# Attention in fixed program order, three units in flight, and weight requests next to the sums that free their buffers

## Chip, cores, metric

One core of one Trainium2 chip. The metric is the time of one execution on the device, in microseconds (us), as the median of several runs. Kernels of one call run on the same chip and share the runs of the kernel before.

## The reference

```python
def phi(x):                                   # 64 -> 256 features
    proj = einsum('bhsd,df->bhsf', x, w_phi)
    proj = proj - max(abs(proj), axis=-1)
    return concatenate([exp(proj), exp(-proj)], axis=-1)
q_p, k_p = phi(q), phi(k)                     # 8 batches, 8 heads, 576 rows, 64 columns
kv  = einsum('bhsf,bhsd->bhfd', k_p, v);  z = sum(k_p, axis=2)
x   = (q_p @ kv) / (q_p @ z + 1e-6)           # -> (8, 576, 512)
X   = rfft(x, axis=1)[:, :64]                 # 64 modes
Y   = X * (w_r + i w_i)                       # one 512x512 complex matrix for each mode
u   = x + irfft(Y, n=576)
out = u + relu(u @ w_ch)
```

The weights `w_r` and `w_i` are 134 MB of fp32 in HBM. They are cast to bf16 on the way in, so 67 MB land.

## The kernel before

Attention runs in 16 units: 4 groups `g` of two heads, times 4 pairs `bp` of batches. When a group's four units are done, its 128 channels are in frequency form, and 16 "sums" (calls of `mix`) of four modes each can run. There are 64 sums, and each consumes one weight tile of 2 x 512 KB. So the first sum can run only after unit 3.

```python
pw_cm  = tc.tile_pool(name="pw", bufs=7)      # weight tiles, 1 MB each
pin_cm = tc.tile_pool(name="pin", bufs=2)     # q, k, v of a unit
pm_cm  = tc.tile_pool(name="pm", bufs=2)

def load(g, bp):                              # 12 DMA requests
    ...
    for t, src, eng in ((kb, k, nc.gpsimd), (vn, v, nc.sync), (qb, q, nc.gpsimd)):
        for i in range(2):
            hs = src[2 * bp + i, 2 * g:2 * g + 2]
            eng.dma_start(t[:, 8*i:8*i+8, :]..., hs[:, 0:512, :].rearrange("h (p c) d -> p h (c d)", c=4))
            eng.dma_start(t[64*i:64*i+64, 16:18, :], hs[:, 512:576, :].rearrange("h p d -> p h d"))

def keys(st):       # transpose k, project, abs-max (DVE), two exponentials (ACT), weigh v (DVE), key sums (PE)
    ...
def queries(st, XT): # the same for q, then numerator and denominator, then the forward transform into XT
    ...
def wload(g, mg):
    wt = pw.tile([128, 2, MG, DMODEL], BF16, name="wt", tag="wt")
    for i, w in ((0, moe_w_r), (1, moe_w_i)):
        nc.gpsimd.dma_start(wt[:, i], w[mg*MG:(mg+1)*MG, g*128:(g+1)*128, :].rearrange("m p e -> p m e"))
    return wt

for n, u in enumerate(units):
    g, bp = u
    if n + 2 < len(units):
        st[units[n + 2]] = load(*units[n + 2])
    next_w(2 if g == 0 else 3)                # ask for two or three weight tiles
    if n + 1 < len(units):
        keys(st[units[n + 1]])
    ...
    queries(st.pop(u), XTb[g % 2])
    for _ in range(3):                        # three sums a unit, once there are any
        if mixq:
            mix(*key, wts.pop(key), ...)
    ...
# after attention: one sum, one weight request and two "channel" chunks (x @ w_ch) a turn;
# then the output stage
```

The scheduler decides the order of each engine's instructions. It need not be the program's.

Of the kernel before, what the change touches and what calls it, by code (L numbers as in the profile page):

```python
# [20 lines left out]
NG = 4  # L21
# [5 lines left out]

@with_exitstack
def kernel(
# [13 lines left out]
    nc = tc.nc  # L43

# [20 lines left out]
    pw_cm = tc.tile_pool(name="pw", bufs=7)  # L65
# [7 lines left out]
    def load(g, bp):  # L73
        kb = pin.tile([128, 18, D_], BF16, name="kb")
        qb = pin.tile([128, 18, D_], BF16, name="qb")
        vn = pin.tile([128, 18, D_], F32, name="vn")
        for t, src, eng in ((kb, k, nc.gpsimd), (vn, v, nc.sync), (qb, q, nc.gpsimd)):
            for i in range(2):
                b = 2 * bp + i
                hs = src[b, 2 * g:2 * g + 2]  # L80
                eng.dma_start(  # L81
                    t[:, 8 * i:8 * i + 8, :].rearrange("p (h c) d -> p h (c d)", h=2),
                    hs[:, 0:512, :].rearrange("h (p c) d -> p h (c d)", c=4),
                )
                eng.dma_start(
                    t[64 * i:64 * i + 64, 16:18, :],
                    hs[:, 512:576, :].rearrange("h p d -> p h d"),
                )
        return dict(g=g, bp=bp, qb=qb, kb=kb, vn=vn)


    wpf = const.tile([128, 128], F32, name="wpf")
    nc.sync.dma_start(wpf[0:64, :], w_phi)
    nc.sync.dma_start(wpf[64:128, :], w_phi)
    si = const.tile([128, 5], I32, name="si")
    nc.gpsimd.iota(si[:, 0:4], [[1, 4]], base=0, channel_multiplier=4)
    nc.gpsimd.iota(si[0:64, 4:5], [[1, 1]], base=512, channel_multiplier=1)
    nc.gpsimd.iota(si[64:128, 4:5], [[1, 1]], base=512, channel_multiplier=1)
    mi = const.tile([128, 64], I32, name="mi")
    nc.gpsimd.iota(mi, [[4, 2], [8, NO], [1, 4]], base=0, channel_multiplier=0)  # L100

    st = {(0, 0): load(0, 0)}
# [4 lines left out]
    nc.vector.tensor_copy(ident_b, ident_f)  # L107
    w2blk = const.tile([128, 256], BF16, name="w2blk")
    nc.vector.memset(w2blk, 0.0)
    nc.vector.tensor_copy(w2blk[0:64, 0:128], wpf[0:64, :])  # L110
    nc.vector.tensor_copy(w2blk[64:128, 128:256], wpf[64:128, :])

    CF = const.tile([128, 6, 4, 64], BF16, name="CF")
# [3 lines left out]
    nc.vector.tensor_copy(sf, si)  # L117
    mf = const.tile([128, 64], F32, name="mf")
    nc.vector.tensor_copy(mf, mi)

    def sc(i):
        return yacc[:, 2 * i:2 * i + 2, :].rearrange("p a e -> p (a e)")[:, 0:640].rearrange(
            "p (c r m) -> p c r m", c=5, r=2)

    ang, rnd, csf = sc(0), sc(1), sc(2)
    nc.vector.tensor_tensor(
# [5 lines left out]
    nc.vector.tensor_scalar_add(out=ang[:, :, 0, :], in0=ang[:, :, 1, :], scalar1=S_ / 4.0)  # L132
    MAGIC = 8388608.0
    nc.vector.tensor_scalar(
        out=rnd, in0=ang, scalar1=1.0 / S_, scalar2=MAGIC, op0=ALU.mult, op1=ALU.add)
    nc.vector.tensor_scalar(
        out=rnd, in0=rnd, scalar1=-MAGIC, scalar2=-float(S_), op0=ALU.add, op1=ALU.mult)
    nc.vector.tensor_tensor(out=ang, in0=ang, in1=rnd, op=ALU.add)
    nc.scalar.activation(csf, ang, ACT.Sin, scale=2.0 * math.pi / S_)

    def tables():

        nc.vector.memset(CF[:, 4:6], 0.0)
        for p0, p1, d, n in ((0, 128, 0, 4), (0, 64, 4, 1), (64, 128, 5, 1)):
            src = csf[p0:p1, min(d, 4):min(d, 4) + n]
            dst = CF[p0:p1, d:d + n]
            nc.vector.tensor_copy(dst[:, :, 0, :], src[:, :, 0, :])
            nc.vector.tensor_scalar_mul(out=dst[:, :, 1, :], in0=src[:, :, 1, :], scalar1=-1.0)
            nc.vector.tensor_copy(dst[:, :, 2, :], src[:, :, 1, :])
            nc.vector.tensor_copy(dst[:, :, 3, :], src[:, :, 0, :])  # L150

        cio = yacc[:, 6:8, :].rearrange("p a e -> p (a e)")[:, 0:640].rearrange(
            "p (c m t r) -> p c m t r", c=5, t=2, r=2)
        for r in range(2):
            for t in range(2):
                nc.vector.tensor_scalar_mul(
                    out=cio[:, :, :, t, r], in0=csf[:, :, r, 32 * t:32 * t + 32],
                    scalar1=(2.0 - 4.0 * r) / S_)
        for c in range(5):
            nc.vector.tensor_scalar_mul(  # L160
                out=cio[:, c, 0, 0, :], in0=cio[:, c, 0, 0, :], scalar1=0.5)
            pct = one([128, 128])
            nc.tensor.transpose(pct, cio[:, c].rearrange("p m t r -> p (m t r)"), ident_f)
            nc.vector.tensor_copy(CI[:, c, :], pct)

    def transposed(src, name):

        dst = pm.tile([128, 9, 128], BF16, name=name, tag="xT")
        flat = src.rearrange("p n d -> p (n d)")
        ptr = two([128, 9, 128], BF16)  # L170
        for j in range(9):
            nc.tensor.transpose(ptr[:, j, :], flat[:, j * 128:(j + 1) * 128], ident_b)  # L172
        nc.scalar.copy(dst, ptr)  # L173
        return dst

    def absmax(tT, m, by_head):

        for i in range(2):
            ps = two([128, 8, 128])
            for j in range(4):  # L180
                if by_head:
                    o = ps[:, 2 * j:2 * j + 2, :]
                else:
                    h, cc = j // 2, j % 2
                    o = ps.rearrange("p (c h) f -> p c h f", h=2)[:, 2 * cc:2 * cc + 2, h, :]
                nc.tensor.matmul(o, lhsT=tT[:, 4 * i + j, :],  # L186
                                 rhs=w2blk.rearrange("p (c f) -> p c f", c=2),
                                 start=True, stop=True)
            nc.vector.tensor_reduce(  # L189
                out=m[:, 8 * i:8 * i + 8], in_=ps, axis=AX.X, op=ALU.max,  # L190
                apply_absolute_value=True,
            )
            yield i, ps
        ps = one([128, 2, 128])
        nc.tensor.matmul(
            ps.rearrange("p h f -> p (h f)"), lhsT=tT[:, 8, :], rhs=w2blk,
            start=True, stop=True,
        )
        nc.vector.tensor_reduce(
            out=m[:, 16:18], in_=ps, axis=AX.X, op=ALU.max, apply_absolute_value=True,  # L200
        )
        yield 2, ps

    def keys(st):
        kT = transposed(st["kb"], "kT")
        mk = pm.tile([128, 2, 18], F32, name="mk")
        ABs = [pm.tile([128, 2, 8, 128], BF16, name="AB", tag="AB", bufs=3) for _ in range(2)]
        ABr = pm.tile([128, 2, 2, 128], BF16, name="ABr")
        for i, ps in absmax(kT, mk[:, 1], True):
            dst = ABs[i] if i < 2 else ABr  # L210
            nc.scalar.activation(dst[:, 0], ps, ACT.Exp, scale=1.0)  # L211
            nc.scalar.activation(dst[:, 1], ps, ACT.Exp, scale=-1.0)  # L212
        nc.vector.tensor_scalar_mul(out=mk[:, 0], in0=mk[:, 1], scalar1=-1.0)
        ee = pm.tile([128, 2, 18], F32, name="ee")
        nc.scalar.activation(ee, mk, ACT.Exp)
        va = pm.tile([128, 2, 18, 65], BF16, name="va")
        nc.vector.tensor_copy(va[:, :, :, 64], ee)
        for ab in range(2):
            nc.vector.tensor_tensor(  # L219
                out=va[:, ab, :, 0:64], in0=st["vn"],  # L220
                in1=ee[:, ab, :].unsqueeze(2).to_broadcast([128, 18, 64]), op=ALU.mult,
            )
        kvz = pm.tile([128, 2, 4, 65], BF16, name="kvz")
        for i in range(2):
            pk = one([128, 4, 65])
            for h in range(2):
                for ab in range(2):
                    o = pk[:, 2 * h + ab, :]
                    for c in range(4):
                        nc.tensor.matmul(  # L230
                            o, lhsT=ABs[i][:, ab, 4 * h + c, :],
                            rhs=va[:, ab, 8 * i + 4 * h + c, :],
                            start=(c == 0), stop=False,
                        )
                    r = slice(64 * i, 64 * i + 64)
                    nc.tensor.matmul(  # L236
                        o, lhsT=ABr[r, ab, h, :], rhs=va[r, ab, 16 + h, :],
                        start=False, stop=True,
                    )
            nc.scalar.copy(kvz[:, i], pk)  # L240
        st["kvz"] = kvz

    def queries(st, XT):
        g, bp, kvz = st["g"], st["bp"], st["kvz"]
        qT = transposed(st["qb"], "qT")
        mq = pm.tile([128, 18], F32, name="mq")
        for _ in absmax(qT, mq, False):
            pass
# [166 lines left out]
    for n, u in enumerate(units):  # L415
# [6 lines left out]
        if n == 0:  # L422
            tables()
# [93 lines left out]
```

## Time and profile before

| stage (us) | what runs | DMA landed |
|---|---|---|
| 30 to 76 | attention, first weights | 213 GB/s |
| 76 to 138 | attention alone, all seven weight buffers full | 61 GB/s |
| 138 to 364 | attention with three sums a unit | 188 GB/s |
| 364 to 503 | the other 28 sums, waiting for weights | 207 GB/s |
| 503 to 550 | output | 206 GB/s |

The median is 545.87 us (544.34 to 549.05, 3 runs).

From the page of the kernel before: the busy share of each of 40 equal slices in tenths (DMA), what the DMA engines moved, and the two DMA queues that matter. POOL issues q0 (q, k and the weights) and SP issues q1 (v and the output). The last column is the time that the packets took, as a share of 16 engines' span.

```profile
span 550.3 us, 8008 instructions
DMA  9699993343999999999999999799999999995466
GB/s 166 87 225 204 215 140 60 64 49 65 206 189 210 135 218 178 160 213 180 214 218 215 181 181 184 117 204 206 206 206 206 212 216 213 215 213 99 163 267 267
q0 software_dynamic: 94736, 77.09, 90.0%
q1 hardware_dynamic: 17568, 21.04, 12.6%
```

The hole in slices 5 to 9 is the stretch from 76 to 138 us. The next view is the busy time of each engine in given stretches of the kernel before. It ends with the granted share of the TensorE clock, the DMA share and the GB/s. A DMA share above 1 means that packets overlap on an engine: in full stretches it is 1.22 to 1.27.

```profile
core 0: us, PE busy (x) PEld busy (x) DVE busy (x) ACT busy (x) POOL busy (x), PEclk, DMA share, GB/s
30.00:76.00 46.00, 32.77 (x279) 23.31 (x279) 27.38 (x49) 26.61 (x42) 20.65 (x30) 0.81 1.27 213
76.00:138.00 62.00, 44.25 (x412) 30.25 (x413) 37.61 (x63) 34.53 (x56) 18.26 (x28) 0.67 0.41 61
138.00:364.00 226.00, 164.80 (x1631) 108.14 (x1643) 143.37 (x243) 132.45 (x205) 90.26 (x129) 0.76 1.16 188
364.00:503.00 139.00, 86.28 (x562) 37.49 (x566) 25.39 (x51) 29.55 (x51) 34.08 (x46) 0.82 1.22 207
503.00:550.30 47.30, 38.38 (x160) 15.42 (x160) 25.01 (x37) 22.29 (x38) 0.00 (x0) 0.86 0.54 206
```

Between 76 and 138 us no engine is full: PE is busy 44 of 62 us, DVE 38, ACT 35. The units wait on the chain through the engines. The chain of work that ended last, in order of time (start, duration, what), shows it there for the kernel before:

```profile
113.25 1.11 DVE mk L189
114.39 1.02 ACT AB L211
115.41 0.66 ACT AB L212
...
119.31 1.02 ACT qT L173
120.38 1.03 PE two L186 x4
```

After attention the same chain is weight DMA alone:

```profile
364.12 0.73 POOL wt L327
364.85 19.23 DMA wt<-in_moe_w_i_dram
384.37 20.05 DMA wt<-in_moe_w_i_dram
404.70 20.05 DMA wt<-in_moe_w_i_dram
```

### The profile page before, as it was taken

The page shows a single profiled execution, that of the slowest core. Times are in us where ns is not written, and L with a number is a line of the kernel's source. Part 1 is how long each engine was busy: PE and PEld are TensorE (multiplying, and loading weights), DVE is VectorE, ACT ScalarE, POOL GpSimd, SP SyncE. Part 2 cuts the span into 40 slices and gives each one's busy share as a digit, 9 for nine tenths or more (in the row PEclk, how much of TensorE's full clock was granted, in tenths as well). Part 3 has the DMA queues.
Part 4 walks back from the last instruction along what each step waited for, and adds up shares of the span by engine and source line. Part 5 has one row for each costly group of instructions (what it writes and reads, how often), then busy time and mean ns, then how long its engine had stood idle before and what let it go on. Part 6 is the DMA issues. An engine that isn't in the chain of part 4 may idle for free.

```text
span 550.3 us, 8008 instructions
## 1 busy us (share of the span) xinstructions
PE 376.5 (68%) x3103; PEld 221.7 (40%) x3133; DVE 279.7 (51%) x486; ACT 256.5 (47%) x403; POOL 186.8 (34%) x273
## 2 busy tenths in 40 slices
PE   2377767658667666778768677787766774345995
PEld 1255545445445444455445354343333331111342
DVE  7647485584555764566965665662222220000574
ACT  3346555655565566567665565312221331011463
POOL 8853331133432715626242533143223222200000
PEclk9999575775675897678975777799989996565899
DMA  9699993343999999999999999799999999995466
GB/s 166 87 225 204 215 140 60 64 49 65 206 189 210 135 218 178 160 213 180 214 218 215 181 181 184 117 204 206 206 206 206 212 216 213 215 213 99 163 267 267
DMA packets 112341, 98.63 MB, mean 179 GB/s; under 512 B 17968, under 2 KB 110768, under 8 KB 111280
## 3 DMA queue, kind: packets, MB, share of 16 engines
q0 software_dynamic: 94736, 77.09, 90.0%
q1 hardware_dynamic: 17568, 21.04, 12.6%
q8 instruction: 24, 0.39, 0.3%
q14 instruction: 13, 0.11, 0.1%
HBM read 163.64 MB, written 9.44 MB: 314 GB/s over the span
## 4 chain that ended last, share of the span: by engine, by line
PE 41%; DMA 23%; ACT 18%; DVE 12%; issue 4%; POOL 2%; DVEq 0%; POOLq 0%; ACTq 0%
DMA wt<-in_moe_w_i_dram 15%; DMA wt<-in_moe_w_r_dram 8%; PE two L186 7%; PE one L230 6%; ACT AQ L263 5%; PE one L236 5%; PE one L344 5%; ACT AB L211 4%; PE pt L466 3%; ACT AB L212 3%; PE one L283 3%; DVE mk L189 3%; PE one L312 3%; PE pt L468 3%; ACT qT L173 2%
## 5 line engine op out<-in xcount | busy, mean ns | idle before, releaser
L327 POOL DMA_DIRECT2D wt<-in_moe_w_r_dram x64 | 48.9, 764 | 93.3 <-PE one L344 37.4
L263 ACT ACTIVATE AQ<-two 128x1024 bf16<-128x1024 f32 x64 | 61.6, 1027 | 14.8 <-PE two L186 6.1
L327 POOL DMA_DIRECT2D wt<-in_moe_w_i_dram x64 | 49.0, 765 | 48.7 <-DMA wt<-in_moe_w_i_dram 44.7
L81 POOL DMA_DIRECT2D kb<-in_k_dram x32 | 23.6, 736 | 78.4 <-PE one L283 32.7
L394 ACT CAST xw<-one 128x512 bf16<-128x512 f32 x36 | 21.1, 585 | 62.0 <-PE one L392 54.9
L230 PE MATMUL one<-va,AB 128*128 128x65 bf16 x512 | 48.2, 231 | 2.6 <-DVE va L219 2.6
L392 PE MATMUL one<-wchb,xT 128*128 128x512 bf16 x137 | 39.7, 408 | 13.9 <-DVE xT L389 13.5
L186 PE MATMUL two<-w2blk,qT 128*128 128x256 bf16 x128 | 30.2, 386 | 26.4 <-ACT qT L173 26.3
L211 ACT ACTIVATE AB<-two 128x1024 bf16<-128x1024 f32 x32 | 32.9, 1028 | 31.4 <-DVE mk L189 24.6
L283 PE MATMUL one<-kvz,AQ 128*128 128x65 bf16 x512 | 35.2, 226 | 15.5 <-ACT AQ L263 13.8
L344 PE MATMUL one<-wt,XT_70 128*32 128x512 bf16 x256 | 28.7, 524 | 24.1 <-DMA wt<-in_moe_w_i_dram 14.4
L189 DVE TENSOR_REDUCE mk<-two 128x8 f32<-128x1024 f32 x32 | 42.1, 1493 | 4.7 <-PE two L186 4.7
L389 DVE COPY xT<-one 128x512 bf16<-128x512 bf16 x36 | 15.3, 424 | 56.4 <-PE one L387 56.3
L219 DVE TENSOR_TENSOR va<-vn,ee 128x1152 bf16<-128x1152 f32 x32 | 42.0, 1356 | 0.0
L189 DVE TENSOR_REDUCE mq<-two 128x8 f32<-128x1024 f32 x32 | 38.9, 1218 | 4.2 <-PE two L186 4.0
L283 PEld LDWEIGHTS <-AQ 128*128 128x128 bf16 x512 | 28.8, 120 | 28.4 <-ACT AQ L263 22.9
L312 PE MATMUL one<-CF,xs 128*128 128x256 bf16 x160 | 30.0, 309 | 13.1 <-DVE xs L303 12.1
L81 POOL DMA_DIRECT2D qb<-in_q_dram x32 | 23.4, 731 | 43.5 <-PE two L172 24.3
L230 PEld LDWEIGHTS <-AB 128*128 128x128 bf16 x512 | 32.4, 119 | 10.5 <-issue 3.2
L212 ACT ACTIVATE AB<-two 128x1024 bf16<-128x1024 f32 x32 | 33.0, 1032 | 0.0
L344 PE MATMUL one<-wt,XT_69 128*32 128x512 bf16 x256 | 26.5, 465 | 7.0 <-DMA wt<-in_moe_w_i_dram 5.8
L172 PE MATMUL two<-ident_b,kb 128*128 128x128 bf16 x144 | 18.1, 280 | 19.0 <-DVE ident_b L107 8.4
(136 smaller groups left out, 716.5 us busy)
## 6 DMA issues: line engine op xcount, KB each, us to landing
wt<-in_moe_w_r_dram POOLq DMA_DIRECT2D x64, 512.0 KB, 14.5
wt<-in_moe_w_i_dram POOLq DMA_DIRECT2D x64, 512.0 KB, 16.2
vn<-in_v_dram SPq DMA_DIRECT2D x32, 256.0 KB, 6.7
out_dram<-of SPq DMA_DIRECT2D x8, 1024.0 KB, 3.9
kb<-in_k_dram POOLq DMA_DIRECT2D x32, 128.0 KB, 5.5
qb<-in_q_dram POOLq DMA_DIRECT2D x32, 128.0 KB, 5.8
vn<-in_v_dram SPq DMA_DIRECT2D x32, 32.0 KB, 7.3
XT_69<-yst SPq DMA_DIRECT2D x8, 128.0 KB, 6.1
```

The source lines that it names most:

```text
L81: eng.dma_start(t[:, 8 * i:8 * i + 8, :].rearrange("p (h c) d -> p h (c d)", h=2), hs[:, 0:512, :].rearrange("h (p c) d -> p h (c d)", c=4),)
L186: nc.tensor.matmul(o, lhsT=tT[:, 4 * i + j, :], rhs=w2blk.rearrange("p (c f) -> p c f", c=2), start=True, stop=True)
L189: nc.vector.tensor_reduce(out=m[:, 8 * i:8 * i + 8], in_=ps, axis=AX.X, op=ALU.max, apply_absolute_value=True,)
L211: nc.scalar.activation(dst[:, 0], ps, ACT.Exp, scale=1.0)
L212: nc.scalar.activation(dst[:, 1], ps, ACT.Exp, scale=-1.0)
L219: nc.vector.tensor_tensor(out=va[:, ab, :, 0:64], in0=st["vn"], in1=ee[:, ab, :].unsqueeze(2).to_broadcast([128, 18, 64]), op=ALU.mult,)
L230: nc.tensor.matmul(o, lhsT=ABs[i][:, ab, 4 * h + c, :], rhs=va[:, ab, 8 * i + 4 * h + c, :], start=(c == 0), stop=False,)
L263: nc.scalar.activation(AQ[:, ab], ps, ACT.Exp, scale=1.0 - 2.0 * ab)
L283: nc.tensor.matmul(pn[ab][:, n - n0, :], lhsT=AQs[i][:, ab, c % 2, 2 * h + c // 2, :], rhs=kvz[:, i, 2 * h + ab, :], start=True, stop=True,)
L312: nc.tensor.matmul(px[:, :, i, :], lhsT=xs[:, g, bp, n:n + 2, :].rearrange("p h d -> p (h d)"), rhs=CF[:, c if c < 4 else 4 + i], start=(c ...
L327: nc.gpsimd.dma_start(wt[:, i], w[mg * MG:(mg + 1) * MG, g * 128:(g + 1) * 128, :].rearrange("m p e -> p m e"),)
L344: nc.tensor.matmul(py[32 * j:32 * j + 32, :], lhsT=XT[:, s0:s0 + 4, :, 32 * t + 4 * o + j].rearrange("p r b -> p (r b)"), rhs=wt[:, i, j, ...
```

## The change

The intent is threefold. Attention is cut into small steps and written in a fixed order on every engine. In step `n` the queries of unit n, the keys of unit n+1 and the transposes of unit n+2 are interleaved, so that a producer and its consumer have other work between them. Weight tiles are asked for right behind the sum that frees their buffer. The stock of weights before the first sum also grows from 7 to 13: an eighth pool buffer, and five tiles in memory that is not in use yet. The code calls those five `held`; I call them borrowed homes below.

```diff
+class InOrder:                                  # each call is kept in program order
+    def __getattr__(self, name):
+        ...
+            return self.tc.keep_in_program_order(ins) if self.on else ins
+pe, dve, act = (InOrder(tc, e) for e in (nc.tensor, nc.vector, nc.scalar))
+pool, sp = InOrder(tc, nc.gpsimd), InOrder(tc, nc.sync)
-    pw_cm = tc.tile_pool(name="pw", bufs=7)
+    pw_cm = tc.tile_pool(name="pw", bufs=8)
 ...
+    def home(g, mg):                             # the five borrowed homes
+        if g == 0 and mg < 2:            t = yacc...            # accumulator of the sums
+        elif g == 0 and mg == 2:         t = XTb[1]...
+        elif g == 0 and mg in (10, 11):  t = xs[:, mg - 8]...   # attention output of groups 2, 3
+        else:
+            return pw.tile([128, 2, MG, DMODEL], BF16, name="wt", tag="wt")
 ...
+    def some(n):
+        for _ in range(n):
+            if mixq:
+                key = mixq.pop(0)
+                mix(*key, wts.pop(key), XTb[key[0] % 2])
+                ...
+                if key not in held:
+                    next_w(1)                    # the request behind its sum
+    for n in range(-1, len(units) + 1):
+        P, Q, K, R = (unit(n + i) for i in (-1, 0, 1, 2))
+        X = 0 if n < 4 else 6 if n == 4 else 4 if n % 2 else 2    # sums in this step: 42 in all
+        Q.cols_q(0); Q.exp_q(0); K.rows_k(0); K.exp_k(0)          # (tests for None cut)
+        Q.kv(0); Q.kv(1); Q.cols_q(1); Q.exp_q(1); P.freq(); Q.num(0)
+        K.turn_q(); unit(n + 3).load_q(); K.rows_k(1); K.exp_k(1)
+        next_w(2) if n < 3 ...; some(min(X, 2)); Q.num(6); Q.cols_q(2); Q.exp_q(2); some(min(X - 2, 2))
+        K.rows_k(2); K.exp_k(2); K.weigh_v(); K.rows_q(0); K.rows_q(1); K.rows_q(2)
+        R.turn_k(); unit(n + 4).load_k(); K.weigh_v2(); unit(n + 3).load_v(); Q.num(12); K.exp_mq()
+        if n == -1: forward_table()
+        if n == 0:  inverse_table()
+        ...; some(X - 4)
-            rl = pb.tile([128, DMODEL], F32, name="rl", bufs=3)
+            rl = pb.tile([128, DMODEL], F32, name="rl")
```

Cut: the methods of a unit, which hold the same operations as `keys` and `queries` before. Only the copy out of a transpose is new: it is split in two. Some buffer counts and memories differ as well (three buffers instead of two for a transposed q or k, the transposes in smaller PSUM tiles, one buffer for `va`), and the first loads are issued in another order.

## The prediction

> **What bounds the kernel now.** The 16 DMA engines are the resource to fill. The page gives 98.63 MB moved at a mean of 179 GB/s; the busy-time table by stretch gives 205 to 215 GB/s wherever the DMA share saturates (425 to 478 us: 213). Weights are read as fp32 and land as bf16, so 213 GB/s landed is about 426 GB/s read. The Trainium skill, page "DMA: Bandwidth & Descriptors", section "Specifications", gives a fabric ceiling of 435 GB/s; the trace agrees, so I take 213 as the limit.
>
> Stages (chain of waits in order of time, and the table by stretch):
> - 0 to 364 us: attention with 36 of 64 weight sums. From 76 to 138 us DMA moves only 61 GB/s: all seven weight buffers are full and no sum can run before unit 4. Attention takes 20.7 us a unit there, although DVE is busy 12 to 13, ACT 12 and PE 15 us of it. From 138 us on, about 21.5 us a unit at 188 GB/s.
> - 364 to 503 us: the other 28 sums, 5.0 us each, waiting for DMA (207 GB/s).
> - 503 to 550 us: output, PE busy 38 of 47 us. The diff only shrinks one pool there.
>
> **What the change does.** Arithmetic and bytes stay. Every engine follows program order; step n works on the queries of unit n, the keys of n+1 and the transposes of n+2, with independent work between producer and consumer, so the unit should fall toward its busiest engine, 16.5 to 18.5 us. Stock before the first sum rises from 7 MB to 13 MB (8 pool buffers, 5 borrowed homes). A weight request stands right behind the sum that frees its buffer; sums within attention rise from 36 to 42, requests from at most 43 to 50. Added: each transpose's eviction is split in two (two 1.15 us evictions a unit become four, estimated +0.4 us ACT a unit), off the critical path if DMA bounds.
>
> **Critical path, as an estimate.** The stock moves 6 MB into the idle stretch, 6/0.213 = 28 us of DMA time. Units 4 to 15 need 3 weights plus 1.18 MB of q, k, v each: 4.2 MB/0.213 = 19.7 us against 21.5, some 20 us more. Floor: about 87.5 MB before the output at 213 GB/s is 411 us, plus 3 us start, 5 us last sum, 47 us output: 466 us. In-order PE stalls, POOL blocked on one buffer, and 206 instead of 213 GB/s in the channel stage will cost about 15 us: attention ends near 342 to 350 us, the last weight lands near 428, end near 481.
>
> **Predicted: 481 us**, range 463 to 504. Faster by over 2%: 0.96; within 2%: 0.03; slower: 0.01.
>
> **Signs.** Right: the 61 GB/s hole is gone, at least 190 GB/s in nearly every slice from 30 us to the output; first sums near 95 to 105 us; unit period 17 to 18 us early, about 20 later; the wait stretch after attention 75 to 90 us instead of 139; output still 46 to 48 us. The granted clock may rise above 0.6 in early units, since the skill's page "TensorE: Matmul & The Clock Gate", Part 1, says activity releases the throttle. Wrong: units over 20 us early, or DMA holes inside attention.
>
> **What would make it wrong.** The fixed order may stall PE behind a late exponential or a weight, holding units at 21 us: then about 500. POOL's single order may hold q and k behind a weight request. Or the output stage slows with two buffers instead of three.

## The result, and the profile after

The changed kernel takes 488.78 us (487.16 to 492.07, 4 runs) against 547.46 us for the kernel before in the same runs. The ratio is 0.893, with a 95% interval of 0.884 to 0.902. A ratio here is the mean time of one kernel's fast runs over that of the other's of the same rounds, so it is not quite the ratio of the medians.

The same lines of the page, of the changed kernel:

```profile
span 488.5 us, 8037 instructions
DMA  9999999999999999999999999999999999992576
GB/s 170 193 216 216 203 214 206 200 203 155 218 218 213 143 205 213 183 204 207 210 190 176 218 165 205 206 207 206 207 206 214 213 213 217 213 214 45 226 296 252
q0 software_dynamic: 94736, 77.09, 100.5%
q1 hardware_dynamic: 17568, 21.04, 14.5%
```

The hole is gone but for a dip from 108 to 120 us. DMA is at 90% or more from the second slice until the output stage, and the mean rises from 179 to 202 GB/s. The start is better too: the second slice moves 193 GB/s instead of 87. The stretches of the changed kernel:

```profile
30.00:76.00 46.00, 29.95 (x293) 21.17 (x294) 32.82 (x64) 27.05 (x46) 20.25 (x29) 0.78 1.27 210
76.00:138.00 62.00, 48.69 (x540) 34.21 (x544) 51.05 (x85) 45.07 (x80) 33.07 (x49) 0.88 1.23 196
138.00:325.00 187.00, 139.06 (x1474) 96.19 (x1483) 132.49 (x219) 115.84 (x197) 78.48 (x112) 0.79 1.21 197
325.00:442.00 117.00, 76.70 (x528) 34.98 (x539) 24.33 (x51) 29.31 (x51) 26.72 (x36) 0.92 1.22 209
442.00:488.50 46.50, 37.57 (x161) 15.22 (x163) 25.22 (x37) 22.56 (x38) 0.00 (x0) 0.87 0.55 209
```

In the same 62 us, 76 to 138, DVE does 51 us of work instead of 38, and DMA moves 196 GB/s instead of 61. The last unit's frequency form is written at 327.5 us (before: 366.1 us).

The lines of the chain that ended last in the changed kernel show two things. Early, it goes through the compute engines, one unit after the other. From about 217 us on it is DMA, inside attention too: even a k load stands in the queue behind weights for 12.7 us.

```profile
37.51 2.62 DVE va L38 x3
...
62.91 2.63 DVE va L38 x3
...
80.44 2.62 DVE va L38 x3
...
97.40 2.63 DVE va L38 x3
...
222.23 21.39 DMA wt<-in_moe_w_i_dram
...
248.54 12.67 DMA kb<-in_k_dram
...
266.89 21.75 DMA wt<-in_moe_w_i_dram
```

(`va` is v weighed by the keys, once a unit. L38 is the line of the in-order helper, so all attention has that line.) Of the first nine distances from one `va` to the next, eight are 16.8 to 18.8 us; one is 25.4 us, between the first two lines of this fence. The last six are 18.2 to 20.4 us and, where PE waits for k, 26.8 us.

**What the packets cost.** The bytes are the same in both kernels, yet the rate inside attention, 197 GB/s, is below that of pure weights, 206, at the same DMA share. Counting the trace's packets of the changed kernel by size explains it:

```
landed size, what          packets   mean ns   sum over 16 engines, us
 128 B  q, k tails (cast)     8192     31.8      16.3
 512 B  q, k (cast)          16384     60.7      62.2
1024 B  weights, w_ch (cast) 66048     98.8     407.9
 256 B  v tails               4096     29.0       7.4
1024 B  v, and y and z       10240     58.0      37.1
2048 B and 8192 B  output     1536      -        24.2
```

A cast packet reads twice what lands. By bytes read, the packets of 256 B, 1 KB and 2 KB take about 30, 60 and 99 ns. So a packet costs some 20 ns plus 37 to 40 ns a KB (the output's 8 KB packets, 321 ns, fit too; its 2 KB packets, 114 ns, lie above), and q and k are dear for their bytes. Without the output the sum is 538 us of 16 engines, with some 6 us of 4-byte packets (18 ns each) that the table leaves out. (The two lines of the page say the same: 115.0% of 488.5 us, less 24 us.) At the overlap of 1.24 that DMA reaches when it is full (the median of 2 us pieces before the last weight lands) that is 433 us. With 3 us of start and 46 us from the last weight to the end, this is an estimated floor of 482 us, and the changed kernel is 6 us above it. The estimate leans on the overlap: with 1.22, the mean from 30 to 442 us, it would be 490 us, so the 6 us are no firm number. The same sum from the trace of the kernel before (540 us of 16 engines, 47 us of output) gives 486 us, and that kernel is some 60 us above.

### The profile page after: what moved, and what is told of

It is laid out like the page before. It is cut to its first block, busy times and chain, and to the rows that moved or that the text cites. A ratio compares the mean times of both kernels' runs of the same rounds, so it can differ in the third digit from the quotient of the medians.

```text
span 488.5 us, 8037 instructions
## 1 busy us (share of the span) xinstructions
PE 347.6 (71%) x3104; PEld 212.3 (43%) x3133; DVE 284.4 (58%) x492; ACT 256.8 (53%) x435; POOL 181.7 (37%) x267
## 4 chain that ended last, share of the span: by engine, by line
DMA 40%; DVE 23%; PE 22%; ACT 5%; issue 4%; POOL 3%; another core or an unknown queue 0%; DVEq 0%; SPq 0%; ACTq 0%; POOLq 0%
DMA wt<-in_moe_w_i_dram 28%; PE one L38 12%; DMA wt<-in_moe_w_r_dram 9%; DVE va L38 6%; DVE mq L38 4%; PE pt L596 4%; DVE nd L38 4%; DVE mk L38 4%; DMA kb<-in_k_dram 3%; DVE xs L38 3%; PE two L38 3%; POOL wt L38 3%; PE pt L598 3%; ACT AB L38 2%; DVE rd L38 1%
## 5 line engine op out<-in xcount | busy, mean ns | idle before, releaser
L38 ACT ACTIVATE AB<-two 128x1024 bf16<-128x1024 f32 x64 | 62.1, 1022 | 50.7 <-DVE mk L38 50.3
L38 ACT ACTIVATE AQ<-two 128x1024 bf16<-128x1024 f32 x64 | 62.5, 1038 | 18.0 <-PE two L38 12.3
L38 POOL DMA_DIRECT2D wt<-in_moe_w_r_dram x59 | 44.7, 758 | 66.8 <-DMA wt<-in_moe_w_r_dram 29.1
L38 POOL DMA_DIRECT2D qb<-in_q_dram x64 | 42.2, 666 | 73.4 <-DMA wt<-in_moe_w_i_dram 31.1
L38 POOL DMA_DIRECT2D wt<-in_moe_w_i_dram x59 | 44.5, 754 | 53.9 <-DMA wt<-in_moe_w_i_dram 48.8
L38 PE MATMUL one<-va,AB 128*128 128x65 bf16 x512 | 45.8, 223 | 17.5 <-DVE va L38 17.3
L38 POOL DMA_DIRECT2D kb<-in_k_dram x64 | 42.3, 672 | 38.3 <-DMA wt<-in_moe_w_i_dram 17.9
L38 DVE TENSOR_REDUCE mk<-two 128x8 f32<-128x1024 f32 x32 | 39.0, 1219 | 5.8 <-PE two L38 5.8
L38 DVE TENSOR_TENSOR va<-vn,ee 128x1152 bf16<-128x1152 f32 x32 | 42.0, 1355 | 0.0
L38 PEld LDWEIGHTS <-AB 128*128 128x128 bf16 x512 | 29.1, 112 | 27.3 <-DVE va L38 11.9
L38 DVE TENSOR_REDUCE mq<-two 128x8 f32<-128x1024 f32 x32 | 37.7, 1217 | 1.4 <-PE two L38 1.4
L38 PE MATMUL one<-kvz,AQ 128*128 128x65 bf16 x512 | 29.6, 205 | 6.9 <-ACT kvz L38 2.7
L38 PE MATMUL one<-ident_b,kb 128*128 128x128 bf16 x144 | 14.4, 244 | 25.3 <-DMA kb<-in_k_dram 24.4
L38 PEld LDWEIGHTS <-AQ 128*128 128x128 bf16 x512 | 25.7, 105 | 15.1 <-issue 12.1
L38 PE MATMUL one<-CF,xs 128*128 128x256 bf16 x160 | 30.9, 364 | 1.7 <-DVE xs L38 1.7
L38 PE MATMUL one<-wt,XT_70 128*32 128x512 bf16 x256 | 22.5, 427 | 13.0 <-DMA wt<-in_moe_w_i_dram 8.9
L38 DVE TENSOR_TENSOR nd<-one,nd 128x390 f32<-128x390 f32 x48 | 27.1, 565 | 5.4 <-PE one L38 0.5
L609 DVE TENSOR_TENSOR of<-pt,rl 128x512 f32<-128x512 f32 x32 | 21.8, 690 | 13.8 <-ACT rl L607 13.4
L38 PE MATMUL two<-w2blk,qT 128*128 128x256 bf16 x128 | 19.8, 289 | 13.0 <-ACT AB L38 10.6
```

The source lines that it names most:

```text
L38: ins = f(*args, **kwargs)
L609: nc.vector.tensor_tensor(out=o, in0=ps[0], in1=rl, op=ALU.add)
```

## The experiments

Theory A: the DMA engines are the limit, so the time is the packets' time plus the output stage, plus whatever time they stand idle before the last weight. Theory B: the pace of the compute engines sets the time, and DMA follows. Beside these two there are the parts of the change: fixed order, step structure, stock, and place of the request.

| run | median us | ratio to before, 95% interval |
|---|---|---|
| after_again (control) | 489.21 | 0.892 (0.886 to 0.899) |
| stock8 | 509.87 | 0.929 (0.921 to 0.937) |
| late_request | 490.68 | 0.894 (0.889 to 0.899) |
| no_tails | 476.61 | 0.869 (0.864 to 0.874) |
| free_order | 492.09 | 0.895 (0.889 to 0.900) |
| before_fixed | 820.18 | 1.490 (1.479 to 1.501) |
| before_stock12 | 548.48 | 0.992 (0.982 to 1.002) |
| before_sums4 | 529.41 | 0.967 (0.961 to 0.973) |
| before_half | 502.86 | 0.914 (0.906 to 0.921) |
| after_half | 456.41 | 0.834 (0.830 to 0.839) |
| big_kv | 478.75 | 0.874 (0.868 to 0.880) |
| big_kv_tables | 471.32 | 0.862 (0.859 to 0.864) |

### after_again: the control

> Control: the changed kernel once more, on the chip of the other runs of this call. All theories: 488 us, ratio to before 0.885 to 0.90. Theory A (the DMA engines are full, so the time is the DMA packets' time plus the output stage) and theory B (the pace of the compute engines sets the time, and DMA follows) differ only in the other runs.

As expected: 489.21 us.

### stock8: without the borrowed homes

```diff
-        if g == 0 and mg < 2:          # and likewise for mg == 2 and mg in (10, 11)
+        if g < 0 and mg < 2:
-    held = [(0, mg) for mg in (0, 1, 2, 10, 11)]
+    held = []
-            next_w((2, 2, 2, 2)[n + 1]) ... next_w((1, 2, 0)[n + 1])
+            next_w((2, 2, 1, 0)[n + 1]) ... next_w((1, 0, 0)[n + 1])
```

> The changed kernel without the five borrowed homes: 8 weights in stock before the first sum, not 13; nothing else moved. Theory A: the DMA work asked for before the first sum (8 weights at 5.1 us, q, k and v of some 7.5 units at 5.8 us) is 84 us, the first sums come near 105 us, so DMA stands idle for 15 to 20 us that nothing gives back: 503 to 508 us, with a hole near 90 to 105 us in the profile. Theory B: no sum waits for a weight, 488 us, unchanged.

Measured: 509.87 us, 21 us over the control. The stretches of this run show the hole where theory A put it:

```profile
30.00:76.00 46.00, 31.34 (x277) 21.55 (x276) 30.50 (x60) 26.03 (x44) 18.71 (x28) 0.70 1.22 196
76.00:112.00 36.00, 27.96 (x282) 19.16 (x280) 28.55 (x47) 25.52 (x44) 12.24 (x19) 0.76 0.43 67
112.00:341.00 229.00, 164.20 (x1764) 113.45 (x1760) 156.47 (x260) 137.63 (x236) 98.79 (x141) 0.78 1.24 204
```

At a share of 0.43 instead of 1.24, 36 us lose 24 us of DMA time, and 21 of them show in the time. Theory B, which foresaw no change, fails here.

### late_request: requests at the end of the step

```diff
                 if key not in held:
-                    next_w(1)
+                    owed.append(key)
 ...
         some(X - 4)
+        next_w(len(owed)); owed.clear()
```

> The changed kernel with all weight requests of a step gathered at the step's end instead of each behind its sum; order, stock and sums unchanged. If asking next to the sum matters, requests come on average half a step (8 us) later and in bursts, and DMA runs dry between bursts: 495 to 505 us. If the up to 4 MB already in the queue cover it: within 1% of 488 us. Theory B: 488 us.

Measured: 490.68 us, no difference to the control that these runs resolve. But the queue does not cover the delay everywhere. From 108 to 120 us, around the first sums, DMA's share falls to 0.52 (first line), where the control only dips to 0.96 (second line):

```profile
108.00:120.00 12.00, 9.89 (x129) 7.55 (x131) 9.16 (x17) 10.06 (x19) 5.12 (x9) 0.93 0.52 61
108.00:120.00 12.00, 9.94 (x113) 6.50 (x112) 11.45 (x20) 8.81 (x18) 8.00 (x12) 0.88 0.96 136
```

That is 4 us of DMA time by these shares, of which 1.5 us shows in the medians. So the place of the request is worth little time here, although DMA does feel it.

### no_tails: the smallest packets taken away (wrong result)

```diff
-            eng.dma_start(t[64*i:64*i+64, 16:18, :], hs[:, 512:576, :]...)     # for q and k
+        dve.memset(t[:, 16:18, :], 0.0)
```

> The changed kernel without the 64-row tails of q and k (1.05 MB landed, 8192 packets of 128 bytes; zeroes in their place, so a wrong result on purpose). In the trace these packets take 16.3 us of 16 engines, at the 1.24-fold overlap of the saturated stretches 13 us. Theory A with the cost per packet: 475 us. Theory A with the cost per byte (213 GB/s): 483 us. Theory B: 487 to 488 us.

Measured: 476.61 us, 12.6 us under the control (relative error 0.024, as meant). The cost per packet said 13 us, the cost per byte 5. One per cent of the bytes took 2.6% of the time. That it is so close to 13 is partly luck: all packets together fell by 21 us of 16 engines, or 17 us of DMA time, and a hole took some of it back:

```profile
104.00:116.00 12.00, 10.93 (x123) 7.63 (x123) 8.28 (x17) 9.12 (x15) 2.61 (x4) 0.80 0.36 75
```

The run also takes away 64 small requests and the time that POOL needs to issue them, which it does not separate from the packets. The Trainium skill, page "DMA: Bandwidth & Descriptors", section "Issuing engines are not separate DMA queues", says that DMAs of all issuing engines run on the same 16 engines and interleave; that is why v's packets, which SP issues, stand in the same sum. No run here tests it across issuers: q, k and the weights all come from POOL.

### free_order: the new program, order left to the scheduler

```diff
-        self.tc, self.engine, self.on = tc, engine, True
+        self.tc, self.engine, self.on = tc, engine, False
```

> The changed program without the fixed order: the scheduler places the instructions of each engine as it did in the kernel before; steps, stock and request points as in the program. If the step structure and the stock are what count: within 2% of 488 us. If the fixed order is what holds the units at 17.5 us: the scheduler pulls producers and consumers together again, units near 20 us and DMA holes, 500 to 515 us.

Measured: 492.09 us, ratio 0.895 against the control's 0.892, with intervals that overlap almost wholly. The two kernels' instructions do differ in order on PE, DVE, ACT and POOL. The units take as long (19.3 us on average in both, from the first `va` to the last), and DMA stays full from 76 to 138 us:

```profile
76.00:138.00 62.00, 50.88 (x573) 35.95 (x574) 45.39 (x80) 46.70 (x79) 32.15 (x47) 0.83 1.23 198
```

So the fixed order is not what brings the gain; any effect is below what these runs resolve.

### before_fixed: the old program, order fixed

```diff
+    fixed.tensor, fixed.vector, fixed.scalar, fixed.gpsimd, fixed.sync = (
+        InOrder(tc, e) for e in (real.tensor, real.vector, real.scalar, real.gpsimd, real.sync))
```

> The kernel before with its attention in fixed program order on every engine, and nothing else of the change. Its program puts each consumer right behind its producer, so PE should stand waiting for ACT and DVE: units of 28 us or more, 600 us or more. If fixed order alone brought the gain: under 520 us.

Measured: 820.18 us. The longest waits of this run (engine, what it was about to do, what it waited for: us in total, times, longest):

```profile
POOL wt L38 <- PE one L38: 372.6, 18, 43.4
...
DVE mk L38 <- PE two L38: 162.9, 16, 15.9
PE one L38 <- DVE va L38: 112.3, 32, 6.3
...
PE two L38 <- DMA kb<-in_k_dram: 77.5, 20, 10.2
```

The program of before puts each consumer right behind its producer. Only a scheduler that reorders it makes it usable. A second cause is POOL, whose order is fixed too: it stands before weight requests that wait for sums, and PE waits 77.5 us in all for k. The run does not separate the two. Fixed order is bearable once the program is written in interleaved steps; by itself it costs half as much again.

### before_stock12: the old attention with the larger stock

```diff
+    def home(g, mg): ...                   # the borrowed homes of the changed kernel
-        next_w(2 if g == 0 else 3)
+        next_w(0 if n == 4 else 3)         # 12 weights in the first four units
```

> The kernel before with five borrowed homes as well as its seven buffers: 12 weights asked for in the first four units instead of 8; attention and its scheduling as before. Theory A: the idle DMA stretch of 76 to 138 us is filled with about 5 MB, 5 times 5.1 us: 516 to 525 us. Theory B: 546 us, since the units keep their 20.7 us and no sum comes earlier.

Measured: 548.48 us, no gain that these runs resolve. Theory A as I had put it fails here: it promised 516 to 525 us. The stretches of this run:

```profile
76.00:108.00 32.00, 23.92 (x231) 16.63 (x231) 19.30 (x35) 18.64 (x29) 14.26 (x22) 0.69 1.24 203
108.00:160.00 52.00, 35.48 (x327) 24.07 (x328) 31.25 (x53) 30.50 (x46) 15.67 (x23) 0.67 0.53 83
160.00:200.00 40.00, 30.23 (x301) 20.35 (x304) 25.11 (x42) 22.18 (x37) 15.60 (x24) 0.74 1.08 178
200.00:230.00 30.00, 19.15 (x174) 12.58 (x173) 15.49 (x26) 18.86 (x28) 10.80 (x17) 0.72 0.59 83
230.00:364.00 134.00, 100.18 (x1010) 64.18 (x1017) 89.75 (x155) 74.04 (x115) 50.05 (x71) 0.80 1.15 188
364.00:503.00 139.00, 84.92 (x544) 36.74 (x553) 24.52 (x49) 30.06 (x52) 32.66 (x44) 0.81 1.20 204
```

The old hole is filled until 108 us, and then it opens again at 108 to 160 and at 200 to 230 us. A sum whose weight lies in a borrowed home frees no pool buffer. After the homes are used up, requests can be ahead of the sums only by the seven buffers, and the sums keep the pace of the old attention. The requests bear it out. In the kernel before, 84 of the 128 half tiles had been asked for when attention ended at 366 us; in this run too, 84 (74 in the pool and 10 in the homes) by 364 us. From the last frequency form to the last sum it takes 136 us in both (366.1 to 502.4, 364.0 to 500.4). So the stock was given back before attention ended.

This edit has a mistake. Unit 4 writes its frequency form into `XTb[1]` before the sum that reads the weight tile (0, 2) from there: in the trace the write is at 132.2 us, and six of that sum's eight matmuls come after it, at 132.9 us and later. So one of the 64 sums is wrong. It stays within the tolerance, as the whole of before_half does with half of its weights wrong. It costs that sum a wait of 2.6 us and changes no request. before_sums4 has the same mistake; the changed kernel, where that sum runs at 110.1 us and unit 4 writes at 126.1 us, does not.

### before_sums4: larger stock and four sums a unit, old attention

```diff
-        next_w(0 if n == 4 else 3)
+        next_w(3 if n < 4 else 1 if n == 4 else 4)
-        for _ in range(3):                 # sums a unit
+        for _ in range(4):
-        for _ in range(2):                 # channel chunks a sum, after attention
+        for _ in range(3):
```

> The kernel before with the 12-weight stock and four sums a unit instead of three from unit 4 on (48 within attention instead of 36), requests to match, three channel chunks a sum in the stage after; attention and scheduler as before. The stock alone gave nothing, and I think because requests during attention cannot outrun sums, and sums keep the old pace. If that is so, more sums must let the DMA run full through attention (attention end near 375 us, 16 sums left): 490 to 510 us, without any fixed order or new step structure. If the old attention's pace itself is what costs, the added PE work only slows it: 540 us or more.

Measured: 529.41 us, 17 to 18 us below the kernel before, between the two expectations. From 156 to 384 us DMA moves 198 GB/s at a share of 1.21, so more sums do let it run nearly full. But the hole at 108 to 156 us (88 GB/s) stays, since the first sum (126.5 us) still comes only when the fourth old unit is done, and the first sums use borrowed homes. This fits both parts of the reading: requests must be able to run (sums), and attention must be quick enough to let the first sum run before the stock is used up. The second part is argued from the hole; no run gives the old program a quicker attention alone.

### before_half and after_half: the compute pace by itself

```diff
-        for i, w in ((0, moe_w_r), (1, moe_w_i)):
+        for i, w in ((0, moe_w_r),):
 ...
-                    rhs=wt[:, i, j, :], ...
+                    rhs=wt[:, 0, j, :], ...
```

> The kernel before with only the real half of each weight loaded and used twice (a wrong result on purpose): 33.5 MB less DMA, all compute kept. Shows the compute pace of the old attention: units stay near 20.7 us, attention ends near 360 us, then 28 sums at PE pace (3.5 us) and 47 us output: about 505 us. It goes with the same edit on the changed kernel, still to run: theory A there expects 420 to 435 us (DMA no longer the limit), theory B 488 us.

> The changed kernel with only the real half of each weight loaded and used twice (a wrong result on purpose): 33.5 MB less DMA, all compute kept. Shows the compute pace of the new attention. Theory A (DMA full): attention 17 to 17.5 us a unit, its end near 310 us, 22 sums at 3.5 us, 46 us of output: 420 to 435 us, against 503 us for the same edit on the kernel before. Theory B (compute pace sets the time already): 488 us.

Measured: 502.86 and 456.41 us. (The results are wrong, although the modes weigh so little in the output that they stay within the tolerance.) Half the weight bytes are worth 48 us in the old kernel (by the runs of the same call; 44 against other calls) and 33 us in the new one. Without the DMA limit the new attention is 46 us quicker than the old. Its units then take 18.7 us on average (from the first `va` to the last, 15 steps) against 20.8.

My 420 to 435 us for the second was too low. I had 17 to 17.5 us a unit and 3.5 us a sum; the trace has 18.7 us a unit, the slow start included, and about 4.2 us a sum (319 to 411 us for 22 sums) with its two channel chunks. So the changed kernel has two floors close together, by these estimates: DMA at 482 us, and compute at 456 us or less, since half of the weights still move in that run. It sits just above the higher one. The old one had 486 us and 503 us, and sat 44 us above the higher, because it met them one after the other: compute pace with DMA idle, then DMA pace with compute idle.

### big_kv: k and v in longer runs

The two heads of a unit lie one behind the other in memory, so 1152 rows can be given to 128 partitions, nine in a row. Key sums then run over the 64 partitions of one head.

```diff
+    def load9(t, src, g, bp, eng):                     # for k and v; q as before
+        for i in range(2):
+            eng.dma_start(t[:, 9*i:9*i+9, :].rearrange("p c d -> p (c d)"),
+                src[2*bp+i, 2*g:2*g+2].rearrange("h s d -> (h s d)").rearrange("(p f) -> p f", p=128))
-        def kv(self, i):                               # one PSUM bank for each batch
+        def kv(self, h):                               # one PSUM bank for each head
+            r = slice(64 * h, 64 * h + 64)
+            for i in range(2):
+                for ab in range(2):
+                    for c in range(9):
+                        n = 9 * i + c
+                        pe.matmul(pk[:, i, ab, :], lhsT=self.AB[n // 8][r, ab, n % 8, :],
+                                  rhs=self.va[r, ab, n, :], start=(c == 0), stop=(c == 8))
```

A first draft kept one bank for both heads. The race check refused it, since the two halves of the rows may write the bank at once; it was not run.

> The changed kernel with k and v loaded in runs of nine rows of one head (two heads lie behind one another in memory, so a partition takes 2304 consecutive floats) instead of four rows and a tail of one; the key sums then run over half the partitions, 72 matmuls a unit instead of 40, one PSUM bank a head. Same bytes, exact result. Theory A with a cost per packet: k's and v's packets fall from about 39 and 37 us of 16 engines to about 22 each (38 ns per KB as the output's 8 KB packets cost), 32/1.24 = 26 us of DMA time less: 462 to 470 us. Theory A with a cost per byte: 488 us. Theory B: 490 to 500 us, since PE has more to do.

(The text is wrong by a unit: nine rows are 576 floats, or 2304 bytes.) Measured: 478.75 us, a correct result, 10 us less than the changed kernel in place of the expected 18 to 26. The new packets take 107.5 and 107.9 ns for 2304 bytes read, 48 ns a KB and not the 38 that I had put in (the 8 KB packets take 40): 20 ns a packet plus 39 ns a KB would have said 108. So k and v fell to 27.5 and 27.6 us of 16 engines, 21 us less; all packets together fell by 23 us, 19 us of DMA time at the overlap of 1.24. Of those 19 us, 10 were realised. Some 6 us of the rest are a hole that had opened (a share of 0.65 instead of 1.24 for 12 us), 86 GB/s from 108 to 120 us: with cheaper k and v, the stock is used up sooner, and the first sums come no earlier.

```profile
108.00:120.00 12.00, 9.90 (x132) 7.23 (x131) 10.21 (x19) 9.59 (x20) 6.02 (x10) 0.97 0.65 86
120.00:312.00 192.00, 152.76 (x1966) 113.78 (x1964) 144.47 (x237) 129.01 (x220) 73.43 (x106) 0.80 1.24 214
```

### big_kv_tables: and the inverse table out of the way

What delays the first sums is the one long step seen above: 25.4 us between two units. The waits of PE in the changed kernel between 30 and 62 us begin with this line:

```profile
PE one L38 <- DVE xs L38: 8.8, 5, 6.8
```

These are the five transposes of the inverse table at the end of step 0 (`xs` is the memory its source is built in). In fixed order PE reaches them long before DVE has built the table, and may do nothing else first.

```diff
         if n == 0:
             inverse_table()                            # now DVE's part only
+        if 0 < n < 4:
+            turn_table(((0, 1), (2, 3), (4,))[n - 1])  # the five transposes, spread
```

> The previous kernel (k and v in nine-row runs) with the five transposes of the inverse table spread over steps 1 to 3 instead of all at the end of step 0. In the traces PE waits 8.8 us there for DVE to reach the table, with nothing else allowed before it by the fixed order; the second unit comes 25 us after the first instead of 17.5. The run in nine-row pieces then still had a DMA hole near 108 to 120 us (86 GB/s), because the stock of 13 ran out before the first sums. If the first sums come 8 us sooner, the hole shrinks by as much: ratio 0.855 to 0.862 to the kernel before, about 470 us (DMA floor from its packets 464). If something else sets the hole: 478 us, ratio 0.874.

Measured: 471.32 us, a correct result. The ratio, 0.862 (0.859 to 0.864), lies at the upper end of the 0.855 to 0.862 expected. The first sum starts at 102.7 us instead of 110.7 in big_kv, the longest distance between two units is 19.2 us, and the hole is closed:

```profile
108.00:120.00 12.00, 8.40 (x143) 6.58 (x143) 8.80 (x15) 7.72 (x14) 4.17 (x7) 1.00 1.16 204
120.00:312.00 192.00, 153.30 (x1942) 112.93 (x1943) 146.28 (x243) 124.76 (x216) 76.05 (x110) 0.80 1.24 213
```

This version beats both kernels: 3.5% below the changed one by the two ratios to the kernel before (0.862 over 0.893, on different chips), 14% below the one before. Its own floor from its packets is an estimated 464 us.

## Why the prediction was right, and where it was not

- **The time, 481 us, against 488.8 measured: inside the range, and the mechanism in the main as predicted.** DMA is the limit, and the gain comes from closing its idle time. The 61 GB/s hole is gone, and stock8 shows it coming back (67 GB/s) with 21 us when the stock is taken away. Measured against a share of 1.24, the kernel before loses 41 us of DMA time from 76 to 138 us, 15 us from 138 us to the end of attention and 9 us in the first 30 us (share 0.86); the changed kernel loses under 1, 5 and 2 us (share 1.15 at the start). These make up about the 59 us gained. The prediction does not name the 7 us at the start; its floor only allows 3 us there.
- **The floor of 466 us was mis-sized.** The step "about 87.5 MB before the output at 213 GB/s is 411 us" charged every byte alike. Packets cost some 20 ns each on top of their bytes. q and k, a tenth of the landed bytes, take 15% of the packet time before the output (78 of 538 us), and the sum is 433 us, not 411. no_tails decided between the two: 12.6 us, where the byte said 5 and the packet 13. The other term, 15 us for stalls and for 206 instead of 213 GB/s in the channel stage, was too large: the kernel is 6 us above the corrected floor, by an overlap of 1.24. The two errors, 16 us too little and 9 too much, cancelled in part, which is luck, and the 8 us left over are about their difference.
- **"The stock moves 6 MB into the idle stretch ... 28 us of DMA time" holds only together with the faster attention.** In the changed kernel five of the tiles are worth 21 us, in the old one nothing that the runs resolve (before_stock12). I had taken a filled hole for a gain. It is one only if DMA is the limit for the rest of attention too; otherwise the same hole opens later.
- **Units: right early, and right in the mean later, but not in where attention ends.** Eight of the first nine take 16.8 to 18.8 us; one takes 25.4 us, which I had not foreseen although the diff shows the table in the fixed order. The mean from the third group's start on is near 20 us, as predicted. First sums at 95 to 105 us: 108.0. Attention end at 342 to 350 us: 327.5. The stretch after it, 75 to 90 us: about 115. Attention ran ahead of the weights; by the reading above, with DMA full, how the same DMA time is divided between the stages does not change the end.
- **"At least 190 GB/s in nearly every slice": mostly.** Of the slices from 30 us to the output, 155, 143, 183, 176 and 165 fall below it. The last three have a DMA share of 1.15 to 1.22 all the same; q and k make up a third of their packet time, against 18% from 30 to 320 us. In the first two q and k make up about half, and their shares, 1.11 and 1.06, leave some idle time as well.
- **The clock.** I cited the Trainium skill, page "TensorE: Matmul & The Clock Gate", Part 1, for activity releasing the throttle. From 76 to 138 us the granted clock is 0.88 instead of 0.67, with PE busy 79% instead of 71%. The trace agrees in that stretch, but PE's busy share alone does not set the clock: from 30 to 76 us in the kernel before, PE is busy 71% too, at 0.81. No run here shows what the clock is worth by itself.
- **The output stage** takes 46.5 us instead of 47.3; the smaller pool costs nothing that shows.
- **What the change is named for is not what pays.** I wrote that every engine follows program order, "so the unit should fall toward its busiest engine". The fall is put down to the steps by elimination, with their buffers and split copies, which no run separates: left to the scheduler, the same program takes 492.09 us (free_order, unresolved from the control). Requests next to their sums are worth nothing that the times resolve (late_request). Of the risks I named, POOL's single order holding k behind weights did happen: 12.7 us once in the chain, and PE waited 15.8 us in all for k from 138 to 325 us. DMA's share was 1.21 meanwhile, so it should have cost little; no run takes it away.

How much each part gives depends on the others. With a stock of 8 the new program is 37 to 40 us better than before; this includes 42 sums instead of 36 and one more buffer, which no run separates in the new program. The larger stock gives another 21. In the old program the stock gives nothing that shows, and stock with more sums gives 17 to 18.

## What to carry to other kernels

Before crediting a filled DMA hole, follow the requests to the end of the stage: if they are bounded by buffers that a slow consumer frees, the hole only moves, and the consumer's pace, not the stock, has to change as well. Size a DMA floor by packets (their count times the time that the trace gives for their size), not by bytes, and measure the compute pace by halving the bytes; a kernel far above both floors may, as here, be meeting them one after the other. Interleaving independent units in the program is what made a fixed order bearable here, and then every late producer in that order, even a table built once, is worth a look.

## What the Trainium skill lacked or had wrong

- "DMA: Bandwidth & Descriptors", section "Why small descriptors are slow (HBM only)", counts the overhead for 256 B, and says of joining descriptors into packets that it is "only worth it at ≤256 B desc size". That section gives no cost by size above 256 B, where longer runs in the layout still pay; other pages of the skill touch on larger sizes, without a series of costs. Here packets that read 256 B, 1 KB, 2 KB and 2304 B took 32, 61, 99 and 108 ns, that is 127, 61, 49 and 48 ns a KB. Runs of 2304 B in place of 1 KB and 256 B for k and v saved 21 us of 16 engines' packet time.
- The same page, section "Specifications", gives ≥512 B as the minimum for line rate. In these traces a packet that reads 1 KB still cost nearly a quarter more for each byte than one of 2 KB (61 against 49 ns a KB).
- The page has no figure for loads that cast fp32 to bf16. A stream of weights alone lands 206 GB/s, which is 412 GB/s read, somewhat below the 435 GB/s ceiling of "Specifications". The read side is what to count: 1 KB read took 61 ns where 512 B landed and 58 ns where 1 KB landed.
